# First-weight pieces of 512 columns, an early touch of the weight, and a gate on k's first exponential, in a fused attention and SiLU kernel

## The chip, the cores and the metric

One core of a Trainium2 chip runs the whole program. The metric is the device time of one execution in microseconds; the time before is the median of seven runs. A profiled execution, taken by the hardware profiler, gives the traces.

## The reference

```
# q, k, v: (8, 8, 576, 64) f32; w_in: (512, 2048); w_out: (2048, 512)
q_s = softmax(q, axis=-1)              # exp / sum over the head's 64 columns
k_s = softmax(k, axis=2)               # exp / sum over the 576 rows
kv  = einsum('bhsd,bhse->bhde', k_s, v)
o   = einsum('bhsd,bhde->bhse', q_s, kv)
x   = o.transpose(0, 2, 1, 3).reshape(4608, 512)
h   = x @ w_in
out = (h * sigmoid(h)) @ w_out         # (4608, 512) f32
```

## The kernel before

**Tiling.** Eight batches of 576 rows go through linear attention; the resulting 4608 rows of x go through the two-layer block in nine chunks of 512 rows (chunk 0's first layer covers the 576 rows of batch 0, as a part i=0 of 320 columns and a part i=1 of 256). The head dimension is packed in two halves, called cc, of four heads each.

**Attention of one batch b.** `load` brings q, k, v as f32 tiles qt, kt, vt. `exp` (L114, ACT) makes eq and ek in bf16. `qsum` (L133, L134, DVE) sums eq and inverts, `qnorm` (L141) multiplies. eq is turned into qT, by TensorE (`tr`, L159) for batch 0 and by a DMA transpose (L151) after that. `vcast` (L123, L125) converts v into vaug, which carries a column of ones, so that `kv` (L178) gives k's sums too. `kvcopy` scales the result into kvn, on DVE (L198) or on ACT (L196), as the plan's `ke` says. `xt` (L220) multiplies kvn and qT, and `xtcopy` (L236, L238) moves the product from PSUM to XT, which holds x transposed.

**The two layers.** For chunk 0 `mm1` (L251) forms one block fb of 128 hidden columns from four matmuls, and `act1` (L281) applies SiLU on ACT into GT. Block fb reads W1 at columns 128 fb to 128 fb + 127. `mm2` (L530) is chunk 0's second layer. Chunk 1 and half of chunk 2 use `mm1` too. The rest of the first layer, and the second layer from chunk 1 on, use a seven-product scheme (`product1`, L344, and `product`, L445), whose sums of inputs are made by `xsum` (XS), `vsum` (TX), `presum` (SW and GT, L400 to L406) and `wsum` (TW), and whose results are joined by `sum1` (L362 to L370) and `after` (L467 to L486).

**Order.** All instructions of an engine run in program order. The start is written out by hand (L554 to L636); after it, a list of steps is sorted by the positions that PLAN, STEADY and their neighbours give: `order` for the first layer, `y` for the second, `act`, `add` for ACT and DVE steps, `pb` for presums, `kc` for kvcopy, and so on. Each chunk has its own plan; chunks 3 to 7 share STEADY.

**Transfers.** q, k, v of batch 0 are issued by SP, in halves: q, q, k, v, k, v. The weights and batch 1's q, k, v are issued by POOL, whose queue writes its descriptors in software and converts the f32 weights to bf16 on the way. `WORDER` is their order; `load_w` issues one. The first weight is cut into six pieces, w10 to w15: four of 256 columns, then two of 512. They are held back by a gate: a copy of one element of vt into a scratch tile on POOL, so that POOL's queue stands until v's first half has landed:

```
WORDER = ['w11', 'w13', 'w10', 'w12', 'w14', 'w15', 'q', 'w21', 'w20', 'k', 'w22', 'v', 'w23']
GATE = ('vt', 0)
```

Before its first products are due, TensorE runs matmuls on a constant tile (`heat`, L591). The first two products of `order`, (3,0) and (2,0), start with the two inner blocks of XT's first half, before the second half is copied.

Of the kernel before, what the change touches and what calls it, by code (L numbers as in the profile page):

```python
# [9 lines left out]
BF16 = mybir.dt.bfloat16  # L10
# [2 lines left out]
AX = mybir.AxisListType  # L13


PLAN = {
    0: {'y': [31.0, 31.5, 33.5, 34.0, 34.0, 34.5, 35.0, 35.5, 36.0, 38.5, 40.0, 41.0, 42.0, 44.0, 45.5, 46.5], 'ex': [28.8, 28.3, 35.8, 30.3], 'qs': [38.0, 36.5], 'qn': [38.51, 38.01], 'vs': [31.5, 39.5], 'ks': [43.0, 40.5], 'kc': [46.01, 43.6], 'lq': 41.5, 'tp': 40.5, 'ox': [47.5, 47.5], 'oc': [47.51, 47.6], 've': [2, 1], 'order': [(3, 0), (2, 0), (0, 0), (0, 1), (3, 1), (5, 0), (6, 0), (4, 0), (2, 1), (1, 0), (7, 1), (1, 1), (11, 1), (8, 1), (6, 1), (12, 0), (11, 0), (14, 0), (10, 1), (4, 1), (12, 1), (7, 0), (8, 0), (5, 1), (13, 0), (10, 0), (9, 1), (13, 1), (15, 1), (9, 0), (15, 0), (14, 1)], 'ke': [1, 0], 'oe': [1, 1], 'qe': [1, 0], 'pad': 16},
    1: {'ex': [15.2, 17.22, 22.74, 19.26], 'qs': [18.0, 18.5], 'qn': [18.01, 19.1], 'vs': [24.0, 20.0], 'ks': [26.0, 22.0], 'kc': [27.01, 26.01], 'lq': 13.5, 'lk': 19.6, 'lv': 22.2, 'tp': 19.5, 'ox': [28.0, 28.0], 'oc': [28.51, 28.51], 've': [2, 2], 'pa': [10.9, 13.5, 14.0], 'pae': [0, 0, 0], 'ke': [0, 0], 'oe': [2, 0], 'std': 4, 'order': [], 'add': {}, 'act': {}, 's1': {0: 1, 1: 0, 2: 0, 3: 1}, 'sl': [2.5, 2.5, 2.0, 6.0, 4.5, 6.0, 6.0, 9.0, 8.0, 9.0, 10.5, 11.0, 12.5, 14.0, 15.0, 15.0], 'xs': [7.3, -20.9, 0.5, -6.5], 'xe': [0, 1, 1, 1], 'pad': 14, 'qe': [1, 0]},
    2: {'std': 2, 'order': [(3, 1), (3, 6), (2, 1), (2, 6), (3, 7), (3, 5), (2, 2), (2, 7), (3, 4), (3, 2), (2, 5), (2, 4), (2, 3), (3, 3)], 'y': [-12.5, -12.5, -11.5, -11.0, -11.0, -10.0, -10.0, -10.0, -9.0, -8.0, -5.5, -2.5, -2.0, -1.0], 'ex': [-1.207, -2.202, -0.08, 1.794], 'qs': [9.4, 3.4], 'qn': [11.41, 6.91], 'vs': [1.42, 11.4], 'ks': [19.4, 19.4], 'kc': [19.41, 19.41], 'lq': 19.95, 'lk': 14.762, 'lv': 26.91, 'tp': 12.9, 'ox': [19.9, 20.4], 'oc': [19.91, 20.91], 'sl': [4.5, 5.0, 2.5, 7.5, 5.0, 6.0, 10.0, 10.5], 'add': {(3, 6): 10.55, (3, 7): 12.55, (3, 3): 22.02, (3, 2): 16.02, (3, 1): 9.55, (3, 5): 13.55}, 'act': {(2, 3): 21.02, (3, 5): 17.02, (3, 3): 22.02, (2, 5): 18.55, (3, 4): 18.55, (2, 2): 18.02, (3, 1): 10.02, (2, 1): 11.55, (2, 6): 12.02, (3, 2): 17.55, (2, 4): 21.02}, 's1': {2: 0, 3: 1}, 'xs': [0.1, 1.1, 8.1, 8.1], 'pa': [19.45, 20.45, 20.95], 'ya': {5: -6.0, 3: 1.0, 4: -2.05}, 'm1': [0, 0], 'pb': [-14.4, -13.8, -13.9, -15.5, -9.5], 'xe': [0, 0, 0, 0], 'pae': [1, 1, 1], 'pbe': [0, 0, 0, 1, 0], 've': [1, 2], 'ke': [0, 1], 'oe': [1, 0], 'qe': [1, 0]},
}  # L20
STEADY = {'std': 0, 'order': [(0, 1), (0, 6), (0, 5), (0, 7), (0, 2), (1, 1), (0, 4), (1, 6), (0, 3), (2, 1), (1, 2), (1, 7), (1, 5), (2, 6), (1, 4), (1, 3), (2, 2), (2, 7), (2, 5), (2, 4), (3, 1), (3, 6), (2, 3), (3, 2), (3, 7), (3, 5), (3, 4), (3, 3)], 'y': [0.5, 1.5, 5.0, 6.0, 9.0, 9.5, 9.5, 12.5, 14.5, 18.0, 19.5, 22.5, 25.7, 28.402], 'ex': [3.798, 1.41, 3.92, 1.297], 'qs': [11.4, 6.9], 'qn': [12.41, 9.91], 'vs': [10.9, 12.92], 'ks': [19.4, 19.4], 'kc': [21.91, 20.41], 'lq': 8.95, 'lk': 23.9, 'lv': 24.41, 'tp': 17.4, 'ox': [23.4, 23.4], 'oc': [24.41, 26.41], 'sl': [], 'add': {(3, 6): 22.02, (0, 3): 8.02, (0, 2): 6.02, (0, 5): 5.02, (2, 2): 20.02, (1, 3): 15.55, (1, 4): 15.55, (2, 7): 17.55, (1, 2): 10.55, (0, 4): 8.02, (1, 1): 6.02, (2, 6): 14.55, (1, 6): 10.55, (3, 1): 20.55, (1, 7): 11.55, (3, 2): 24.02}, 'act': {(0, 2): 4.55, (0, 3): 10.02, (2, 5): 18.55, (0, 4): 9.02, (1, 5): 15.02, (3, 3): 27.404, (1, 3): 18.02, (0, 5): 5.02, (3, 4): 26.55, (1, 4): 17.02, (2, 4): 23.02, (2, 3): 23.02, (0, 6): 4.02, (1, 1): 8.02, (3, 6): 22.55, (0, 1): 2.55, (3, 5): 27.55, (2, 1): 13.02, (3, 2): 23.55, (3, 7): 27.02, (1, 7): 13.55, (2, 6): 15.02, (2, 7): 17.02, (1, 2): 12.55}, 's1': {0: 0, 1: 1, 2: 0, 3: 0}, 'xs': [0.296, 0.298, -0.227, 0.4], 'pa': [19.95, 27.407, 27.41], 'pb': [1.45, 1.96, 4.45, 5.46, 3.45], 'ya': {6: 8.0, 5: 18.5, 4: 22.95, 3: 28.852, 7: 14.5}, 'm1': [0, 0], 'xe': [0, 0, 1, 1], 'pae': [1, 1, 1], 'pbe': [0, 0, 1, 1, 1], 've': [1, 2], 'ke': [0, 1], 'oe': [0, 0], 'qe': [1, 1]}
for _t in range(3, 8):
    PLAN[_t] = STEADY
PLAN[8] = {'std': 0, 'order': [(0, 1), (0, 6), (0, 2), (0, 7), (1, 1), (0, 5), (0, 4), (0, 3), (1, 6), (1, 2), (1, 7), (1, 5), (1, 4), (2, 1), (1, 3), (2, 6), (2, 2), (2, 7), (2, 5), (3, 1), (2, 4), (2, 3), (3, 6), (3, 2), (3, 7), (3, 5), (3, 4), (3, 3)], 'y': [1.5, 2.0, 5.5, 8.5, 10.0, 11.0, 14.0, 15.0, 19.5, 22.0, 24.5, 25.8, 27.401, 27.406], 'sl': [], 'add': {(2, 7): 17.55, (3, 2): 24.02, (3, 7): 24.55, (3, 4): 26.55, (3, 1): 20.55, (2, 3): 22.55, (0, 2): 3.55, (0, 3): 8.02, (2, 4): 20.55, (1, 4): 14.02}, 'act': {(2, 1): 15.55, (3, 6): 24.02, (3, 4): 26.55, (2, 3): 24.55, (2, 4): 21.55, (1, 7): 14.02, (2, 6): 19.02, (0, 3): 10.02, (1, 5): 12.55, (0, 4): 8.02, (3, 5): 27.403, (1, 4): 15.02, (2, 7): 21.02, (3, 7): 25.55, (1, 6): 10.02, (1, 3): 15.55, (3, 2): 23.55, (2, 2): 19.02, (3, 1): 20.02, (0, 5): 7.55, (1, 1): 6.55}, 's1': {0: 1, 1: 0, 2: 1, 3: 1}, 'xs': [-0.71, -0.208, -0.207, 1.4], 'pa': [24.45, 27.45, 29.429], 'pb': [0.793, 3.96, 10.45, 8.46, 9.45], 'ya': {6: 10.0, 4: 27.401, 7: 15.45, 2: 11.95}, 'm1': [0, 0], 'xe': [0, 0, 1, 0], 'pae': [1, 1, 1], 'pbe': [0, 1, 0, 1, 0]}
PLAN[9] = {'y': [0, 1, 2, 3, 4, 5, 6, 7, 8, 9, 10, 11, 12, 13], 'ya': {}, 'm1': [0, 0], 'pb': [-0.201, -0.2, -0.2, 1.9, 2.9], 'pbe': [0, 0, 0, 0, 0]}
TXAT = [(0, (0, -10.0, 0, 0)), (0, (0, 16.0, 1, 0)), (1, (1, -24.5, 0, 1)), (1, (0, 20.5, 1, 0)), (2, (0, 25.5, 0, 1)), (2, (2, -28.0, 1, 0)), (3, (2, -25.0, 0, 0)), (3, (1, -12.5, 1, 0))]
TWAT = [(1, -7.0, 1), (0, 38.0, 0), (1, 3.5, 0), (0, 46.0, 0), (1, 9.5, 1), (1, 20.5, 0), (1, 10.0, 0), (0, 39.0, 0)]
WORDER = ['w11', 'w13', 'w10', 'w12', 'w14', 'w15', 'q', 'w21', 'w20', 'k', 'w22', 'v', 'w23']
GATE = ('vt', 0)
HV = (1, 0.0, 0)  # L30
JS = 5
STD = 0
START = {'qn': (0, 0), 'h': [3, 3, 2, 2], 'v': 0, 't': (0, 0, 0, 2), 'x': 1, 'o': 0, 'w': 4}

@with_exitstack
def kernel(
# [13 lines left out]
    nc = tc.nc  # L50
# [6 lines left out]
    NC = DM // 128  # L57
# [10 lines left out]
    glob = ctx.enter_context(tc.tile_pool(name="glob", bufs=1))  # L68
# [15 lines left out]
    warm = glob.tile([128, 512], BF16, name="warm")  # L84
    dummy = glob.tile([1, 1], FP32, name="dummy")
    gate = glob.tile([1, 8], FP32, name="gate")

    ld = ctx.enter_context(tc.tile_pool(name="ld", bufs=1))
    ap = ctx.enter_context(tc.tile_pool(name="ap", bufs=2))
# [5 lines left out]
    st = [dict() for _ in range(B)]  # L95
# [13 lines left out]
    def exp(b, src, dst, cc, js=(0, J)):  # L109
        if dst not in st[b]:  # L110
            st[b][dst] = ap.tile([128, J, NG * D], BF16, name=dst, bufs=1)
        js = slice(*js)
        o = st[b][dst][:, js, cc * 128:(cc + 1) * 128].rearrange("p j (g d) -> p j g d", d=D)
        nc.scalar.activation(out=o, in_=jgd(st[b][src], cc)[:, js], func=ACT.Exp)  # L114

    def vcast(b, cc, eng, gs=(0, 2)):
        if gs[0] == gs[1]:
            return
        gs = slice(2 * cc + gs[0], 2 * cc + gs[1])
        o = vaug.rearrange("p j (g e) -> p j g e", e=E1)[:, :, gs, 0:D]  # L120
        i = st[b]["vt"][:, gs, :].rearrange("p g (j d) -> p j g d", d=D)
        if eng is nc.scalar:
            eng.copy(out=o, in_=i)  # L123
        else:
            eng.tensor_copy(o, i)  # L125
# [167 lines left out]
    def xsum(t, i):  # L293
        V = ENG[PLAN[t]["xe"][i]]
        w = width(t)
# [57 lines left out]
    def sum1(t, g, k):  # L353
# [12 lines left out]
        if k == 1:  # L366
            if PLAN[t]["s1"][g]:
                nc.vector.tensor_scalar_mul(out=new("s1"), in0=o, scalar1=1.0)
# [182 lines left out]
    PSB = {"ring": 6, "ops": 2}  # L551


    nc.vector.memset(dummy, 0.0)  # L554
    nc.vector.memset(warm, 0.0)
    nc.scalar.activation(out=dummy, in_=dummy, func=ACT.Exp)
# [9 lines left out]

    def load_w(name):
        if name[:2] == "w1":
            f = slice(*((0, 256), (256, 512), (512, 768), (768, 1024), (1024, 1536), (1536, 2048))[int(name[2])])
            nc.gpsimd.dma_start(  # L570
                out=W1[:, :, f], in_=w_in[:, f].rearrange("(c p) f -> p c f", p=128)
            )
        elif name[:2] == "w2":
            i = int(name[2])
            nc.gpsimd.dma_start(
                out=W2[:, i * 4:(i + 1) * 4, :],
                in_=w_out[i * 512:(i + 1) * 512, :].rearrange("(fc p) o -> p fc o", p=128),
            )
        else:
            load(1, name + "t", {"q": q, "k": k, "v": v}[name], eng=nc.gpsimd)  # L580

    gx = st[0][GATE[0]]
    nc.gpsimd.tensor_copy(gate[:, 0:1], gx[0:1, 2 * GATE[1] + 1, 0:1])
    for name in WORDER[:START["w"]]:
        load_w(name)

    wps = ps.tile([128, 512], FP32, name="wps", tag="ops", bufs=PSB["ops"])

# [7 lines left out]
    for cc in range(2):  # L596
        exp(0, "qt", "eq", cc)
        qsum(0, cc)
        if cc == 0 or not SB["o"]:
            qnorm(0, cc, ENG[SB["qn"][cc]])  # L600
    exp(0, "kt", "ek", 0)
    vcast(0, 0, nc.scalar)
    exp(0, "kt", "ek", 1)
    for js in HALF:
# [77 lines left out]
    for t in range(NCH):  # L682
        p = PLAN[t]
# [4 lines left out]
        else:  # L688
# [4 lines left out]
            for i, (g, m) in enumerate(p["order"]):  # L693
                x = i + 4 * p["std"]
# [9 lines left out]
    for t in range(1, NCH):  # L704
        for i, (m, a) in enumerate(HALVES):
            x = PLAN[t + 1]["y"][i]
# [14 lines left out]
    for t in range(1, NCH):  # L721
# [5 lines left out]
        for i in range(5):  # L727
            n, h = ((0, 1), (1, 1), (2, 1), (3, 0), (3, 1))[i]
# [33 lines left out]
```

## Time and profile before

| | |
|---|---|
| median of 7 runs | 273.75 us (272.12 to 274.76) |
| profiled execution, its own time | 274.76 us |
| its span | 272.9 us |
| TensorE busy | 254.9 us, 93% of the span |
| DVE, ACT, POOL busy | 200.1, 190.3, 146.8 us |
| mean granted TensorE clock | 0.989 |
| DMA | 46.50 MB in 44014 packets, 170 GB/s over the span |
| POOL's queue (software) | 6096 packets, 7.73 MB, 13.4% of 16 engines' span |

A row of a timeline has the start, the duration, the engine, the line in the kernel, the operation, output and inputs, and how many were merged; in brackets stands how long the engine was idle before, and what ended that. In a row of stretches come the stretch, its length, the busy time of TensorE's matmuls, its weight loads, DVE, ACT and POOL (with the number of instructions that began in it), then the granted TensorE clock, the DMA engines' busy share and the GB/s that they wrote. Sizes of the weight transfers are those of the bf16 side: 256 KB for 256 columns.

### The profile page before, as it was taken

How to read it: one execution, taken by the hardware profiler on the slowest of the kernel's cores; microseconds unless marked ns; L12 is line 12 of the kernel's file. 1: busy time of each engine (PE TensorE's matmuls, PEld its weight loads, DVE VectorE, ACT ScalarE, POOL GpSimd, SP SyncE). 2: the span in 40 equal slices, each digit the busy share in tenths (PEclk: the TensorE clock that was granted, in tenths of full speed). 3: DMA queues.
4: the chain of work that ended last, by engine and by line, in shares of the span. 5: the costliest groups of instructions: out<-in, count | busy, mean ns of one | idle time of the engine just before them, and what ended most of it. 6: DMA issues, size and time to landing. Idle time of an engine off the chain costs nothing.

```text
span 272.9 us, 6537 instructions
## 1 busy us (share of the span) xinstructions
PE 254.9 (93%) x2668; PEld 199.0 (73%) x2668; DVE 200.1 (73%) x343; ACT 190.3 (70%) x317; POOL 146.8 (54%) x91
## 2 busy tenths in 40 slices
PE   8659999899898989999999999998999999999992
PEld 3337754355773768888888888886888887888882
DVE  2932548755878877978996899687978578898832
ACT  5666899668858888977997698759975457444300
POOL 1496209033301978884979397849594637603500
PEclk9997999999999999999999999999999999999998
DMA  7799998991598596578655966592442102110324
GB/s 246 279 162 274 251 336 171 290 389 26 174 263 322 54 336 227 191 147 272 233 155 124 303 219 131 127 308 89 101 94 51 39 13 67 41 38 14 80 67 115
DMA packets 44014, 46.50 MB, mean 170 GB/s; under 512 B 18640, under 2 KB 31952, under 8 KB 43984
## 3 DMA queue, kind: packets, MB, share of 16 engines
q1 hardware_dynamic: 37728, 38.22, 48.0%
q0 software_dynamic: 6096, 7.73, 13.4%
q8 instruction: 21, 0.34, 0.5%
q10 hardware_dynamic: 160, 0.13, 0.2%
q14 instruction: 9, 0.07, 0.1%
HBM read 36.70 MB, written 9.44 MB: 169 GB/s over the span
## 4 chain that ended last, share of the span: by engine, by line
PE 53%; DMA 15%; ACT 9%; DVE 8%; issue 6%; POOL 4%; SPq 3%; DVEq 0%; POOLq 0%; ACTq 0%
PE ops L445 21%; PE hps L344 19%; PE hps L251 10%; DMA kt<-in_k_dram 7%; DMA qt<-in_q_dram 3%; DVE zq L133 2%; DMA qT<-eq 2%; DMA W<-in_moe_w_in_dram 2%; ACT eq L114 2%; DVE u L362 2%; ACT L114 2%; ACT ek L114 2%; ACT L281 1%; ACT GT L281 1%; POOL eq L141 1%
## 5 line engine op out<-in xcount | busy, mean ns | idle before, releaser
L445 PEld LDWEIGHTS <-GT 128*128 128x128 bf16 x512 | 49.5, 98 | 8.4 <-issue 2.3
L344 PEld LDWEIGHTS <-TX 128*128 128x128 bf16 x416 | 40.2, 98 | 8.4 <-issue 3.1
L344 PE MATMUL hps<-XS,TX 128*128 128x256 bf16 x312 | 43.3, 273 | 1.7 <-DVE u L362 0.9
L362 DVE SCALAR_TENSOR_TENSOR u<-hps,u 128x512 f32<-128x512 f32 x52 | 35.8, 688 | 8.8 <-PE hps L344 6.1
L362 DVE SCALAR_TENSOR_TENSOR u<-hps,s 128x512 f32<-128x512 f32 x52 | 35.4, 681 | 8.9 <-PE hps L344 8.8
L445 PEld LDWEIGHTS <-SW 128*128 128x128 bf16 x384 | 37.3, 98 | 5.5 <-DVE SW L402 1.0
L251 PE MATMUL hps<-XT,W 128*128 128x320 bf16 (+3 forms) x224 | 37.5, 328 | 3.6 <-DMA W<-in_moe_w_in_dram 2.2
L386 ACT ACTIVATE GT<-u 128x512 bf16<-128x512 f32 x52 | 32.2, 630 | 9.8 <-DVE u L362 9.8
L251 PEld LDWEIGHTS <-W 128*128 128x128 bf16 x224 | 22.4, 101 | 18.3 <-issue 2.8
L406 POOL TENSOR_TENSOR SW<-GT,SW 128x1024 bf16<-128x1024 bf16 x12 | 26.1, 2171 | 14.7 <-DVE SW L402 14.7
L344 PEld LDWEIGHTS <-W 128*128 128x128 bf16 x312 | 30.4, 98 | 4.0 <-issue 0.2
L445 PE MATMUL ops<-TW,SW 128*128 128x256 bf16 x256 | 32.8, 273 | 0.5 <-DVE SW L402 0.5
L141 POOL TENSOR_TENSOR eq<-eq,rzq 128x1152 bf16<-128x1152 bf16 x11 | 23.6, 2144 | 17.7 <-DVE rzq L134 12.5
L445 PE MATMUL ops<-TW,GT 128*128 128x256 bf16 x256 | 32.7, 273 | 0.3 <-DVE u L467 0.3
L133 DVE TENSOR_REDUCE zq<-eq 128x18 f32<-128x1152 bf16 x16 | 21.5, 1342 | 15.6 <-ACT eq L114 15.6
L445 PE MATMUL ops<-W,GT 128*128 128x256 bf16 x256 | 31.7, 273 | 1.3 <-ACT s L475 1.3
L281 ACT ACTIVATE GT<-hps 128x192 bf16<-128x192 f32 (+4 forms) x72 | 26.0, 408 | 7.6 <-PE hps L251 6.3
L344 PE MATMUL hps<-XT,W 128*128 128x256 bf16 x208 | 30.4, 273 | 0.0
L400 POOL TENSOR_TENSOR SW<-GT 128x1024 bf16<-128x1024 bf16 x7 | 14.9, 2126 | 27.6 <-ACT GT L386 19.0
L404 POOL TENSOR_TENSOR GT<-GT 128x1024 bf16<-128x1024 bf16 x12 | 25.5, 2128 | 0.0
L114 ACT ACTIVATE ek<-kt 128x1152 bf16<-128x1152 f32 x16 | 18.4, 1159 | 8.0 <-DMA kt<-in_k_dram 8.0
L386 ACT ACTIVATE GT<-s 128x512 bf16<-128x512 f32 x26 | 16.4, 631 | 10.0 <-DVE s L362 10.0
(79 smaller groups left out, 394.5 us busy)
## 6 DMA issues: line engine op xcount, KB each, us to landing
qt<-in_q_dram SPq DMA_DIRECT2D x6, 1152.0 KB, 5.8
kt<-in_k_dram SPq DMA_DIRECT2D x6, 1152.0 KB, 6.4
vt<-in_v_dram SPq DMA_DIRECT2D x6, 1152.0 KB, 9.6
out_dram<-u SPq DMA_DIRECT2D x34, 64.0 KB, 3.3
W<-in_moe_w_out_dram POOLq DMA_DIRECT2D x4, 512.0 KB, 18.6
out_dram<-u SPq DMA_DIRECT2D x14, 128.0 KB, 2.7
qt<-in_q_dram SPq DMA_DIRECT2D x2, 576.0 KB, 4.1
kt<-in_k_dram SPq DMA_DIRECT2D x2, 576.0 KB, 8.0
```

Of the source, the lines that this page charges most:

```text
L114: nc.scalar.activation(out=o, in_=jgd(st[b][src], cc)[:, js], func=ACT.Exp)
L133: nc.vector.reduce_sum(out=st[b]["zq"][:, cc, js], in_=e, axis=AX.X)
L141: eng.tensor_tensor(out=e, in0=e, in1=r[:, :, :, None].to_broadcast([128, n, 2, D]), op=ALU.mult)
L251: nc.tensor.matmul(out=hps[:, 0:size], lhsT=W1[:, c, fb * 128:(fb + 1) * 128], rhs=XT[t][:, c, off:off + size], start=(c == 0), stop=(c == ...
L281: nc.scalar.activation(out=y, in_=hps[:, h], func=ACT.Silu)
L344: nc.tensor.matmul(out=o[:, f, :], lhsT=l(c, 2 * g + f), rhs=r(c), start=bool(first and f == 0 and c == 0), stop=(c == HK - 1), skip_group ...
L362: nc.vector.scalar_tensor_tensor(out=out, in0=o, scalar=1.0, in1=x, op0=ALU.mult, op1=ALU.add)
L386: nc.scalar.activation(out=y, in_=MP[t, g, x], func=ACT.Silu)
L400: V.tensor_add(S1[:, f], quad(t, 0, f, 1), quad(t, 1, f, 1))
L404: V.tensor_sub(quad(t, 0, f, 1), quad(t, 0, f, 0), quad(t, 0, f, 1))
L406: V.tensor_sub(S4[:, f], quad(t, 1, f, 0), S2[:, f])
L445: nc.tensor.matmul(out=o, lhsT=l(f), rhs=r(f), start=bool(first and (own or a == 0) and f == 0), stop=(f == HF - 1), skip_group_check=True,)
```

## The change

- The first weight is cut into four pieces of 512 columns, issued in the order of their columns.
- POOL's first instruction is a transfer of four columns of the first weight into a tile that nothing reads (`touch`), 512 runs of four elements.
- The gate copies an element of ek's first half, which ACT writes in the first exponential of k, and the gate and the weights' issue are placed behind that exponential in the program.
- The order of chunk 0's first-layer products follows the new pieces: all of fb 0 to 3 first, then 4 to 7, 8 to 11, 12 to 15.
- In STEADY, kvcopy of cc 0 goes from DVE to ACT (`ke`), and one presum's position changes from 5.46 to 4.46 (`pb`). In the program that moves two kvn scalings in each of four chunks.
- In chunk 8's plan one second-layer product comes half a step earlier, one join half a step earlier, one SiLU has a position of its own, and three presums come two steps later. DVE's L406 and L404 thereby stand behind three sums that they stood among.

```
+WCUT = ((0, 512), (512, 1024), (1024, 1536), (1536, 2048))
+WARM = 1
 PLAN[0]:
-  'order': [(3, 0), (2, 0), (0, 0), (0, 1), (3, 1), (5, 0), (6, 0), (4, 0), (2, 1), (1, 0), (7, 1), (1, 1), (11, 1), (8, 1), (6, 1), (12, 0), ...]
+  'order': [(3, 0), (2, 0), (0, 0), (0, 1), (3, 1), (2, 1), (1, 0), (1, 1), (5, 0), (6, 0), (4, 0), (7, 1), (6, 1), (4, 1), (7, 0), (5, 1), ...]
 STEADY:
-  'pb': [1.45, 1.96, 4.45, 5.46, 3.45], 'ke': [0, 1]
+  'pb': [1.45, 1.96, 4.45, 4.46, 3.45], 'ke': [1, 1]
 PLAN[8]:
-  'y': [..., 19.5, ...], 'add': {..., (1, 4): 14.02}, 'pb': [0.793, 3.96, 10.45, 8.46, 9.45]
+  'y': [..., 19.0, ...], 'add': {..., (1, 4): 13.55}, 'act': {..., (2, 5): 20.02}, 'pb': [0.793, 3.96, 12.45, 10.46, 11.45]
-WORDER = ['w11', 'w13', 'w10', 'w12', 'w14', 'w15', 'q', 'w21', 'w20', 'k', 'w22', 'v', 'w23']
-GATE = ('vt', 0)
+WORDER = ['w10', 'w11', 'w12', 'w13', 'q', 'w21', 'w20', 'k', 'w22', 'v', 'w23']
+GATE = ('ek', 0)
-START = {..., 'w': 4}
+START = {..., 'w': 3}
+    if WARM:
+        nc.gpsimd.dma_start(
+            out=touch, in_=w_in[:, 0:4].rearrange("(c p) f -> p c f", p=128)
+        )
     nc.vector.memset(dummy, 0.0)
...
-            f = slice(*((0, 256), (256, 512), (512, 768), (768, 1024), (1024, 1536), (1536, 2048))[int(name[2])])
+            f = slice(*WCUT[int(name[2])])
...
-    gx = st[0][GATE[0]]
-    nc.gpsimd.tensor_copy(gate[:, 0:1], gx[0:1, 2 * GATE[1] + 1, 0:1])
-    for name in WORDER[:START["w"]]:
-        load_w(name)
...
     exp(0, "kt", "ek", 0)
+    gx = st[0][GATE[0]]
+    gx = gx[0:1, 2 * GATE[1] + 1, 0:1] if GATE[0][1] == "t" else gx[0:1, 0, GATE[1] * 128:GATE[1] * 128 + 1]
+    nc.gpsimd.tensor_copy(gate[:, 0:1], gx)
+    for name in WORDER[:START["w"]]:
+        load_w(name)
     vcast(0, 0, nc.scalar)
```

## The prediction

> **What bounds the kernel now.** I read four views: the page's engine shares and slices, the chain of work that ended last, the timelines of the first 40 us by engine, and stretches of 1 us. Two rows of the page first.
>
> ```profile
> PE 254.9 (93%) x2668; PEld 199.0 (73%) x2668; DVE 200.1 (73%) x343; ACT 190.3 (70%) x317; POOL 146.8 (54%) x91
> PEclk9997999999999999999999999999999999999998
> ```
>
> TensorE is busy 93% of the span, so little is left but its holes, and its clock drops once, in the fourth slice (20.5 to 27.3 us). Both edits that look large (weight pieces, gate) lie just ahead of that. The chain in order of time shows what leads there:
>
> ```profile
> 10.31 1.30 POOL gate L583
> 11.61 1.62 POOL W L570 x2
> 13.22 6.35 DMA W<-in_moe_w_in_dram
> 19.62 13.62 PE hps L251 x96
> 33.27 1.75 ACT GT L281 x7
> 35.04 1.28 ACT L114
> ```
>
> Gate, weight issue, weight transfer, first-layer products of chunk 0, their SiLUs, the exponential's table. From 35.04 on ACT is packed until 48.4. TensorE's and ACT's timelines give the price of the late weight:
>
> ```profile
> 16.17 1.26 PE L251 MATMUL hps<-XT,W 128*128 128x320 bf16 x8
> 19.62 16.44 PE L251 MATMUL hps<-XT,W 128*128 128x320 bf16 x120 [2.19 <-DMA W<-in_moe_w_in_dram]
> 18.21 0.77 ACT L281 ACTIVATE GT<-hps 128x320 bf16<-128x320 f32 x2
> 20.37 1.43 ACT L281 ACTIVATE GT<-hps 128x320 bf16<-128x320 f32 x5 [1.39 <-PE hps L251]
> 22.43 0.44 ACT L281 ACTIVATE GT<-hps 128x320 bf16<-128x320 f32 x1 [0.62 <-PE hps L251]
> 23.50 0.44 ACT L281 ACTIVATE GT<-hps 128x320 bf16<-128x320 f32 x1 [0.63 <-PE hps L251]
> 24.55 10.47 ACT L281 ACTIVATE GT<-hps 128x320 bf16<-128x320 f32 x35 [0.62 <-PE hps L251]
> ```
>
> The 8 matmuls of w11 run at once; the third piece, w10, is awaited 2.19 us. ACT idles 1.39 + 0.62 + 0.63 + 0.62 = 3.26 us, first for the stall and then because TensorE runs at half clock:
>
> ```profile
> 0.00:11.50 11.50, 8.02 (x41) 3.47 (x44) 6.45 (x11) 6.14 (x6) 1.92 (x7) 1.00 0.83 301
> 12.00:13.00 1.00, 1.00 (x12) 0.66 (x11) 0.88 (x5) 0.91 (x1) 1.00 (x2) 1.00 0.08 30
> 19.00:20.00 1.00, 0.38 (x3) 0.31 (x4) 0.00 (x0) 0.00 (x0) 0.70 (x2) 1.00 1.39 187
> 22.00:23.00 1.00, 1.00 (x6) 0.54 (x5) 0.00 (x0) 0.44 (x1) 0.40 (x1) 0.50 1.25 205
> ```
>
> The last three columns are clock, DMA share and GB/s written. Clock 0.50 lasts from 21.0 to about 24.4. The 256-column pieces arrive at about 187 GB/s, the 512-column ones at 205; at 12 to 13 us the DMA is empty. The POOL and DVE timelines explain the gate:
>
> ```profile
> 10.28 1.33 POOL L583 COPY gate<-vt 1x1 f32<-1x1 f32 x1 [8.97 <-DMA vt<-in_v_dram]
> 11.55 4.65 POOL L570 DMA_DIRECT2D W<-in_moe_w_in_dram  x6
> 10.21 1.36 DVE L141 TENSOR_TENSOR eq<-eq,rzq 128x1152 bf16<-128x1152 bf16 x1
> ```
>
> **Weight pieces.** w10 now holds fb 0 to 3, all that the first 8 products use (order (3,0), (2,0), (0,0), (0,1), (3,1), (2,1), (1,0), (1,1)). It writes 512 KB: 2.56 us at 205 GB/s. Before, three 256 KB pieces (786 KB, w13 in the middle) had to land first: first bytes near 13.2, landing 19.6. With the same start, w10 lands near 13.2 + 2.6 + 0.5 (the rate is only 113 to 145 GB/s from 15 to 18 us) + 1 (last bytes to release, as 786 KB took 5.4 of 6.35 us) = 17.3. The products could start at 16.17, so a stall of about 1.1 us stays, against 2.19 in mid-stream, and w11 follows 2.6 us later while w10 feeds 4 x 0.53 + 4 x 0.43 = 3.8 us of matmuls (320 and 256 columns at 2.4 columns per ns, as the warm rows run: 4 x 256 columns in 0.44 us). No later piece is awaited. 32 products need 15.4 us: 17.3 to 32.7, against 36.06. The two saved issues (2 x 0.77 us on POOL) shorten nothing, as POOL runs ahead of the transfers. All four pieces end at 13.2 + 10.2 + 0.5 = 23.9, where w15 landed at 26.2 (DVE waits for it): the q, k, v and w_out transfers behind them on POOL's queue come at least 1 us sooner, so ACT's later needs (k at 41.9, v at 44.7) are met even if shifted 2 us.
>
> ACT then sets the end: its 13.55 us of SiLU work before 35.02 can run packed from 18.21 (the SiLU table load, 16.92 to 18.20, hides the stall). Removed: 3.26, less 0.5 us for small waits while TensorE is only just ahead: -2.7.
>
> **The clock.** The row says: a gap of 2.19 us, then 3.4 us at 0.50. The Trainium skill (TensorE: Matmul & The Clock Gate, Part 1) has the clock halved only after an idle window of about 3.4 us. By the rule the drop has another cause and would stay: TensorE's 29th product, which releases the exponential, comes at 17.3 + 13.9 + 1.7 = 32.9, ACT's end moves only to about 33.5, and the sum loses 0.8. By the row a gap half as long is safe, as one of 1.47 us at 10 to 11.5 us left the clock at 1.00. I follow the row.
>
> **Gate.** ek's first half ends at 8.74 + 1.16 = 9.90, v's first half lands at 10.25. So the gate's wait is 0.35 shorter. But its 1.33 us for one element ends 0.04 after the DVE product of 10.21 to 11.57. The skill (SBUF — State Buffer, on the shared port pair) says that a DVE instruction with two SBUF inputs blocks a GpSimd one that reads SBUF; the row agrees, and speaks against the edit: unless the copy starts before 10.21 it is held to 11.6 as before. By the wait alone the weight comes 0.35 sooner, by an escape 1.5, by the lock 0. The margin is 0.3 us and the touch delays k more than q, so I take 0. POOL's queue behind the gate is the weights, then q, k, v loads; all move with it. In the new order nothing else of POOL passes it.
>
> **Touch.** The 4 KB transfer has 512 runs of 16 bytes, first on POOL's queue: about 0.9 us (first weight issue 0.94) ahead of the identity, which TensorE needs at 8.67: hidden. But its packets share the DMA engines with q, k, v, saturated from 2 to 11.5 us, and those have no cover. Nearest row: 18640 packets under 512 B in 7 transposes of 5.5 us, so 512 cost 512 x 7 x 5.5 / 18640 = 1.1 us. Upper end: the software queue's mean, 13.4% x 16 x 272.9 / 6096 = 96 ns a packet, 512 / 16 x 96 = 3.1 us. Lower: -0.2, if it takes the first-issue surplus (0.94 less 0.77) off the weight. I take 1.1 for the last loads, and 0.6 for the DVE chain that leads to XT, since it starts from q's first half, which meets about half the packets.
>
> **Planner edits.** Four chunks move two kvn scalings (0.24 us apart) from DVE to ACT. DVE waits 1.27 us right after them, at 172.4; ACT has a 0.42 us wait two steps later, and xt starts 1.0 us after ACT would be done. Price 0, between -0.3 and +0.3 each. pb 5.46 to 4.46 leaves POOL's order alone: 0. In chunk 8 DVE's L406 and L404 move behind three sums; L404 would end near 242.6, its reader on TensorE starts 242.82: 0, up to +0.5.
>
> **Sum.** -2.7 + 0.6 = -2.1, in a profiled run of 274.76 (span 272.9). Beyond 53 us TensorE is the bound and the loads chain on buffers, so the shift carries. That run is 1.0 above the median of the 7 runs, 273.75; I apply the shift to the median: 271.65.
>
> **Rivals.** (1) Gate escapes the lock and the touch is free (-0.2): -2.7 - 0.2, w10 at 16.2: 270.8. For it: 0.3 us of margin. Against: k is third in the queue. (2) Half the gain is lost: the clock still drops (+0.8) or the touch reaches the XT chain with its full 1.1 (+0.5): -0.8, 273.0. (3) Slower: tiny packets at the start cost like the software queue's, or more. From 2.7 us of delay on q, k, v (84 ns a packet) the whole gain is gone; at half as much again as that mean, about 150 ns (assumed; no row has runs of 16 bytes), it is 4.8 us: +2.1, 275.9. Against: the transposes' packets cost 33 ns per engine by the same row (5.5 x 7 x 16 / 18640). Place: the wait of the first eq and ek on qt and kt.
>
> **Chances.** Likeliest 0.48, rival 1 0.17, rival 2 0.20, rival 3 0.15. Faster by over 0.5% (below 272.4; about what a measurement of this kernel can tell) 0.65, within 0.5% 0.20, slower 0.15. The likeliest case alone spans 270.8 to 272.5 (touch 0.2 to 1.1, waits 0 to 1); 269.9 to 274.4 adds rivals 1 and 2 and the planner's bounds.
>
> **To check.** Right: no TensorE wait on W after the first products, clock 1.00 at 20 to 25 us, ACT's table load near 33 instead of 35.04, a later q landing by about 0.5. Wrong: a gate copy ending well before DVE's second L141 (rival 1), a clock of 0.5 after 18 us (2), eq's first start past 6 us (3), or TensorE waits at kvn or SW in chunks 4 to 8.

## The result, and the profile after

The changed kernel takes 270.6 us (median of 27 runs, 268.45 to 272.86) against 273.26 us for the kernel before (64 runs, 270.86 to 277.56): a ratio of 0.9901, 95% interval 0.9880 to 0.9923, so 1.0% or 2.7 us faster. The medians are of all runs; the ratio leaves out those more than 1.5% above the fastest of their kernel. The forecast was 271.65, with -2.1 us against the median that it had, 273.75. Faster was the side forecast; the case that came true is rival 1 (the gate escapes the lock, the touch is free) more than the likeliest, as the steps below show.

The profiled execution has a span of 267.5 us, 5.4 less than the first profile of the kernel before. That is twice what the medians differ, because both profiles are off their medians: before's execution took 274.76 us where the median is 273.26, after's 269.25 where it is 270.6.

The page's rows for the engines and the clock:

```profile
PE 253.6 (95%) x2668; PEld 198.7 (74%) x2668; DVE 197.7 (74%) x335; ACT 191.4 (72%) x325; POOL 144.0 (54%) x90
PEclk9999999999999999999999999999999999999999
```

The clock's hole in the fourth slice is gone. The chain in order of time (start, duration, what) no longer has the weight in it. It starts with q's transfer, goes through DVE's preparation of XT, and enters the first-layer products at 15.66:

```profile
0.74 3.62 DMA qt<-in_q_dram
...
15.13 0.53 PE o L224 x8
15.66 13.95 PE hps L255 x112
29.61 0.02 issue
29.63 0.88 ACT GT L285 x3
30.51 0.02 issue
30.53 1.28 ACT L118
```

The last row, the table load for the second batch's exponentials, stood at 35.04. I use its start below as the mark of how far chunk 0 has got. The timeline of the same execution, the rows that answer to those shown of before:

```profile
1.25 0.93 POOL L559 DMA_DIRECT2D touch<-in_moe_w_in_dram  x1 [0.80 <-POOLq L754]
9.20 0.18 POOL L607 CAST gate<-ek 1x1 f32<-1x1 bf16 x1 [6.43 <-ACT ek L118]
9.32 3.01 POOL L578 DMA_DIRECT2D W<-in_moe_w_in_dram  x4
10.22 1.36 DVE L145 TENSOR_TENSOR eq<-eq,rzq 128x1152 bf16<-128x1152 bf16 x1
15.59 15.85 PE L255 MATMUL hps<-XT,W 128*128 128x320 bf16 x128
17.64 12.88 ACT L285 ACTIVATE GT<-hps 128x320 bf16<-128x320 f32 x43
```

All 128 matmuls run in one piece of 15.85 us (worked out: 15.4), with no wait on W. ACT's 43 SiLUs run packed; its four gaps, 3.26 us together, are gone. The gate's copy takes 0.18 us, before DVE's L145 begins. By 1 us stretches (clock, DMA share and GB/s written are the last three columns):

```profile
12.00:13.00 1.00, 1.00 (x15) 0.52 (x15) 1.00 (x6) 0.67 (x3) 1.00 (x2) 1.00 1.22 196
19.00:20.00 1.00, 1.00 (x10) 0.80 (x9) 0.00 (x0) 1.00 (x7) 0.75 (x1) 1.00 1.23 203
22.00:23.00 1.00, 1.00 (x10) 0.80 (x9) 0.00 (x0) 1.00 (x6) 1.00 (x1) 1.00 1.09 402
```

The hole in the transfers at 12 to 13 us (share 0.08) is filled, and the weight is through by 22, when q of the next batch (402 GB/s) takes over. That hole belonged to the late gate and not to the pieces: in the second profile of the kernel before, whose gate copy took 0.18 us, the same stretch has a share of 1.42 and 184 GB/s.

### The profile page after: what moved, and what is told of

The parts are those of the page before. It is cut to its first block, busy times and chain, and to the rows that moved or that the text cites. A ratio compares the mean times of both kernels' runs of the same rounds, so it can differ in the third digit from the quotient of the medians.

```text
span 267.5 us, 6537 instructions
## 1 busy us (share of the span) xinstructions
PE 253.6 (95%) x2668; PEld 198.7 (74%) x2668; DVE 197.7 (74%) x335; ACT 191.4 (72%) x325; POOL 144.0 (54%) x90
## 4 chain that ended last, share of the span: by engine, by line
PE 69%; DVE 10%; ACT 8%; DMA 6%; issue 2%; SPq 2%; DVEq 0%; ACTq 0%
PE ops L449 28%; PE hps L348 26%; PE hps L255 11%; DMA kt<-in_k_dram 5%; DVE zq L137 2%; ACT eq L118 2%; ACT L118 2%; ACT ek L118 2%; DVE eq L145 2%; DVE u L366 1%; PE o L224 1%; PE kvps L182 1%; DMA qt<-in_q_dram 1%; ACT L285 1%; SPq L155 1%
## 5 line engine op out<-in xcount | busy, mean ns | idle before, releaser
L255 PE MATMUL hps<-XT,W 128*128 128x320 bf16 (+3 forms) x224 | 35.6, 318 | 1.5 <-ACT GT L285 1.0
L348 PEld LDWEIGHTS <-W 128*128 128x128 bf16 x312 | 30.4, 98 | 4.1 <-issue 0.4
L255 PEld LDWEIGHTS <-W 128*128 128x128 bf16 x224 | 21.8, 98 | 14.9 <-issue 2.6
L145 POOL TENSOR_TENSOR eq<-eq,rzq 128x1152 bf16<-128x1152 bf16 x11 | 23.5, 2138 | 16.2 <-DVE rzq L138 11.0
L404 POOL TENSOR_TENSOR SW<-GT 128x1024 bf16<-128x1024 bf16 x7 | 14.9, 2127 | 27.6 <-ACT GT L390 15.3
L285 ACT ACTIVATE GT<-hps 128x64 bf16<-128x64 f32 (+4 forms) x72 | 25.3, 419 | 4.3 <-PE hps L255 3.0
```

The lines of the kernel that those rows point to most:

```text
L145: eng.tensor_tensor(out=e, in0=e, in1=r[:, :, :, None].to_broadcast([128, n, 2, D]), op=ALU.mult)
L255: nc.tensor.matmul(out=hps[:, 0:size], lhsT=W1[:, c, fb * 128:(fb + 1) * 128], rhs=XT[t][:, c, off:off + size], start=(c == 0), stop=(c == ...
L285: nc.scalar.activation(out=y, in_=hps[:, h], func=ACT.Silu)
L348: nc.tensor.matmul(out=o[:, f, :], lhsT=l(c, 2 * g + f), rhs=r(c), start=bool(first and f == 0 and c == 0), stop=(c == HK - 1), skip_group ...
L404: V.tensor_add(S1[:, f], quad(t, 0, f, 1), quad(t, 1, f, 1))
```

## The experiments

Theory A: the loss is the wait for w10 in mid-stream, and the order and size of the pieces mend it. Rivals: the gate's release does it; the touch does it; the planner's edits do it.

**Each part alone.** The first kernel has only the pieces, their issue order and the product order; the second only the gate on ek. In both the gate and the weights' issue stand behind k's first exponential in the program, as in the changed kernel, against which the edits are shown:

```
 GATE = ('vt', 0)      # pieces_only
-WARM = 1
+WARM = 0
 # STEADY and PLAN[8] as before

 GATE = ('ek', 0)      # gate_only
+WCUT = ((0, 256), (256, 512), (512, 768), (768, 1024), (1024, 1536), (1536, 2048))
 # WORDER, PLAN[0] order, STEADY, PLAN[8] as before; WARM = 0
```

> The kernel before with the four 512-column pieces and the product order that goes with them; gate on vt, no touch, old plan. Theory A (the wait for the first weight and the half clock after it are the loss, and the piece cut alone mends it): no TensorE wait on W after the first products, table load of the first exponential near 32.5 us instead of 35.0, about 2.0 us faster than before. Theory B (the gate's earlier release does it, the cut only follows): gate copy still 1.3 us long, first products wait for w10 until about 17.3, less than 0.8 us gained.

> The kernel before with the gate on ek's first half; six pieces, old order, no touch, old plan. Theory A: the six pieces arrive up to 1.5 us sooner, the 2.19 us wait for w10 shrinks below 1 us and the clock stays at 1.00, so this alone gains about 1.5 us and the two edits do not add up. Theory B: gate copy ends before DVE's second product (0.2 us instead of 1.33) and 2.0 us or more are gained. If a late k makes the gate miss the port, the copy lasts 1.3 us and nothing is gained.

Measured: pieces alone 0.9925 (0.9892 to 0.9958), 270.56 us against 272.63; gate alone 1.0006 (0.9972 to 1.0041), 272.85 us. Their timelines, first the pieces:

```profile
9.96 0.18 POOL L607 COPY gate<-vt 1x1 f32<-1x1 f32 x1 [8.65 <-DMA vt<-in_v_dram]
15.85 15.86 PE L255 MATMUL hps<-XT,W 128*128 128x320 bf16 x128
30.79 1.28 ACT L118 ACT_TABLE_LOAD   x1
```

Then the gate alone:

```profile
9.67 0.18 POOL L607 CAST gate<-ek 1x1 f32<-1x1 bf16 x1 [8.36 <-ACT ek L118]
18.61 15.11 PE L255 MATMUL hps<-XT,W 128*128 128x320 bf16 x120 [1.48 <-DMA W<-in_moe_w_in_dram]
32.69 1.28 ACT L118 ACT_TABLE_LOAD   x1
```

With the pieces there is no wait although the gate is the old one; with the new gate and the old pieces a wait of 1.48 us stays. Theory A holds for the pieces, with their issue order and the product order that goes with them; which of these two orders does how much was not tested. Its guess that the gate alone would gain 1.5 us fell: the old gate, too, lets go at 9.96 here. The clock stayed at 1.00 in the gate kernel despite the wait.

**Each small part taken away.** The changed kernel without the touch (`WARM = 0`), and with the old plans:

> The changed kernel without the touch. Theory A: the touch's packets cost 24 ns each and nothing waits for them, so no difference from the changed kernel (2.7 us faster than before, within 0.5). Theory B: the touch takes a first-use delay (in the changed kernel 3 us pass between its issue and its packets) off the first weight piece; without it w10 comes 1 us or more later than 15.5 and the gain falls below 2 us.

> The changed kernel with the old STEADY and chunk 8 plans (kvn scaling back on DVE, presums back). Theory A: no difference from the changed kernel (2.7 us faster than before, within 0.5), as the moved work lies beside a busy TensorE. Theory B: the planner's edits bring the 0.9 us that the profiled pair differs after chunk 0, so the gain falls to 1.8 us.

Measured: 0.9916 (0.9884 to 0.9948), 270.54 us, and 0.9918 (0.9887 to 0.9949), 270.62 us. Neither part can be told from nothing beside 0.9901; with intervals of this width a part worth less than about 1 us does not show. The timeline without the touch, then the touch's own answer in the changed kernel:

```profile
9.76 3.17 POOL L578 DMA_DIRECT2D W<-in_moe_w_in_dram  x4
16.15 15.85 PE L255 MATMUL hps<-XT,W 128*128 128x320 bf16 x128 [0.26 <-DMA W<-in_moe_w_in_dram]
31.09 1.28 ACT L118 ACT_TABLE_LOAD   x1
```

```profile
DMA to landing us min/median/max: 6.7/6.7/6.7
```

The touch lands 6.7 us after its issue at 1.25. Its 512 packets run from 5.15 to 7.56 us, at 24 ns each in the mean, so they begin when q's first exponential has started already: at 4.38 in both kernels. They do take room on the DMA engines (278 GB/s at 5 to 6 us, against 341 without the touch), but k's first exponential starts at 7.97 to 8.74 us in the seven profiles with the touch and at 7.82 to 8.74 in the seven without. What the touch gives is the first weight issue's surplus: four issues take 3.01 us with it and 3.17 without, 0.16 us. The wait of 0.26 without it is within what other draws of the changed kernel show.

**Order or size of the pieces.** The changed kernel with the six old pieces, issued in the order of their columns:

```
-WCUT = ((0, 512), (512, 1024), (1024, 1536), (1536, 2048))
+WCUT = ((0, 256), (256, 512), (512, 768), (768, 1024), (1024, 1536), (1536, 2048))
-WORDER = ['w10', 'w11', 'w12', 'w13', 'q', ...]
+WORDER = ['w10', 'w11', 'w12', 'w13', 'w14', 'w15', 'q', ...]
-START = {..., 'w': 3}
+START = {..., 'w': 4}
```

> The changed kernel with the six old pieces (256 columns for the first four) issued in the order of their columns. Theory A1 (the order of arrival is what counts: w13 no longer stands between the pieces that the first products need): as fast as the changed kernel, within 0.5 us. Theory A2 (the size counts: 256-column pieces come at 145 to 187 GB/s against 205): the first products wait about 0.6 us for W, the later ones not, and 0.5 to 1.0 us of the gain is lost.

Measured: 0.9944 (0.9906 to 0.9982), 271.43 us against 273.31. Timeline and one stretch:

```profile
17.08 15.85 PE L255 MATMUL hps<-XT,W 128*128 128x320 bf16 x128 [1.03 <-DMA W<-in_moe_w_in_dram]
32.02 1.28 ACT L118 ACT_TABLE_LOAD   x1
```

```profile
17.00:18.00 1.00, 0.92 (x7) 0.69 (x8) 0.00 (x0) 1.00 (x1) 0.42 (x1) 1.00 1.35 172
```

The order counts: it alone takes away the break in mid-stream, and its gain is clear of noise. Of the 2.7 us, 1.9 are there without the larger size by the medians, 1.5 by the ratio. The size probably counts too, but its share of the time is not shown, since the intervals of the two kernels overlap. What the traces show is the rate: from 13 to 18 us this kernel writes 128 to 172 GB/s, and the changed kernel with the old plans (no_plan), whose weights are issued at nearly the same time (10.10 against 10.05 us), 197 to 219. The two pieces of 256 columns reach the products 1.03 us late; there the first one of 512 is not awaited at all (0 to 0.76 us in the four profiles of the changed kernel).

**The port.** The gate of the changed kernel copies from rzq, which DVE finishes just before L145:

```
-    gx = gx[0:1, 2 * GATE[1] + 1, 0:1] if GATE[0][1] == "t" else ...
+    gx = st[0]["rzq"][0:1, 1, 0, 0:1]
```

> The changed kernel, with the gate copying one element of rzq's second half, which DVE writes just before its second normalizing product (L145). Theory A (the port is shared): the copy starts within 0.1 us after L145 does, and lasts until L145 ends, about 1.3 us instead of 0.18; the weights' issue starts near 11.6 instead of 9.3 to 10.1, the first products wait about 1 us for W, and about half of the gain goes (1.0 to 2.0 us faster than before). Theory B (the 1.33 us of the kernel before were something of the first copy on POOL, not the port): the copy lasts 0.2 us, and little is lost.

Measured: 0.9967 (0.9931 to 1.0004), 271.6 us against 273.31.

```profile
10.31 1.36 DVE L145 TENSOR_TENSOR eq<-eq,rzq 128x1152 bf16<-128x1152 bf16 x1
10.34 1.37 POOL L607 COPY gate<-rzq 1x1 f32<-1x1 f32 x1 [7.57 <-DVE rzq L138]
17.15 15.85 PE L255 MATMUL hps<-XT,W 128*128 128x320 bf16 x128 [1.31 <-DMA W<-in_moe_w_in_dram]
32.09 1.28 ACT L118 ACT_TABLE_LOAD   x1
```

The one-element copy starts 0.03 us after L145, and ends 0.04 us after it: 1.37 us instead of 0.18. This bears out what the Trainium skill (SBUF — State Buffer, Who interferes with whom) states of a DVE instruction with two SBUF inputs and a GpSimd one that reads SBUF. The weight then comes 1.31 us late. Of the gain of 2.7 us, 1.7 are left by the medians and 0.9 by the ratio; the interval does not overlap with that of the changed kernel, so a loss is there, but its size is loosely known.

**More profiles of both.** Three more of each kernel, unchanged:

> The kernel before once more, for a second profile of it. If the profile shown first is typical: gate copy 1.3 us, wait for w10 near 2.2 us, clock 0.5 for 3.4 us, table load at 35.0. If it is a slow draw, as its 274.76 against a median of 272.6 to 273.3 suggests: the gate copy may start ahead of DVE's product and take 0.2 us, the wait is near 1.5 us, the clock stays at 1.00 and the table load is near 33 us.

> The changed kernel once more, for a second profile. No wait on W after the first products in any draw, table load at 30.5 to 31.1 us; the gate copy 0.18 us unless k's first half lands after 8.9 us.

> The kernel before, third profile. Theory A (the wait for w10 is there in every draw, the port lock and the half clock only in some): wait 1.5 to 2.2 us, table load 33 us with a gate copy of 0.2 us and a full clock, up to 35 us with a copy of 1.3 us and a clock of 0.5. Theory B (the wait itself comes only with the lock): no wait when the copy takes 0.2 us.

> The kernel before, fourth profile; as for the third. The gate copy lasts 1.3 us exactly where v's first half lets it start after DVE's second L141, and 0.2 us where it starts before.

> The changed kernel, third profile. Theory A: no wait for W above 0.3 us, clock 1.00 to 25 us, table load 30.5 to 31.1 us, gate copy 0.18 us. Theory B: draws with table loads of 32 us or more turn up here as well.

> The changed kernel, fourth profile; as for the third. After chunk 0, the lead over the second profile of the kernel before stays between 2 and 4.5 us.

The three profiles of the kernel before, in this order: the gate copy, the first-layer products with their wait for W, ACT's SiLUs that began after a gap, and the table load:

```profile
9.91 0.18 POOL L583 COPY gate<-vt 1x1 f32<-1x1 f32 x1 [8.60 <-DMA vt<-in_v_dram]
19.08 15.02 PE L251 MATMUL hps<-XT,W 128*128 128x320 bf16 x120 [2.02 <-DMA W<-in_moe_w_in_dram]
19.84 6.11 ACT L281 ACTIVATE GT<-hps 128x320 bf16<-128x320 f32 x21 [1.22 <-PE hps L251]
26.30 6.76 ACT L281 ACTIVATE GT<-hps 128x320 bf16<-128x320 f32 x21 [0.35 <-PE hps L251]
33.08 1.28 ACT L114 ACT_TABLE_LOAD   x1
...
9.86 0.18 POOL L583 COPY gate<-vt 1x1 f32<-1x1 f32 x1 [8.55 <-DMA vt<-in_v_dram]
20.22 14.77 PE L251 MATMUL hps<-XT,W 128*128 128x320 bf16 x120 [3.20 <-DMA W<-in_moe_w_in_dram]
20.97 12.97 ACT L281 ACTIVATE GT<-hps 128x320 bf16<-128x320 f32 x42 [2.41 <-PE hps L251]
33.96 1.28 ACT L114 ACT_TABLE_LOAD   x1
...
9.33 0.18 POOL L583 COPY gate<-vt 1x1 f32<-1x1 f32 x1 [8.02 <-DMA vt<-in_v_dram]
17.44 1.59 PE L251 MATMUL hps<-XT,W 128*128 128x320 bf16 x12 [0.70 <-DMA W<-in_moe_w_in_dram]
19.42 13.35 PE L251 MATMUL hps<-XT,W 128*128 128x320 bf16 x108 [0.39 <-DMA W<-in_moe_w_in_dram]
20.17 11.56 ACT L281 ACTIVATE GT<-hps 128x320 bf16<-128x320 f32 x37 [0.66 <-PE hps L251]
31.75 1.28 ACT L114 ACT_TABLE_LOAD   x1
```

And the changed kernel, its third and fourth profile:

```profile
16.55 15.85 PE L255 MATMUL hps<-XT,W 128*128 128x320 bf16 x128 [0.76 <-DMA W<-in_moe_w_in_dram]
31.48 1.28 ACT L118 ACT_TABLE_LOAD   x1
...
15.97 15.86 PE L255 MATMUL hps<-XT,W 128*128 128x320 bf16 x128 [0.29 <-DMA W<-in_moe_w_in_dram]
30.91 1.28 ACT L118 ACT_TABLE_LOAD   x1
```

All eight side by side (us):

| | gate copy | wait for W | table load | span |
|---|---|---|---|---|
| before 1 (shown first) | 1.33 | 2.19 | 35.04 | 272.9 |
| before 2 | 0.18 | 2.02 | 33.08 | 271.8 |
| before 3 | 0.18 | 3.20 | 33.96 | 271.1 |
| before 4 | 0.18 | 0.70 + 0.39 | 31.75 | 268.9 |
| after 1 (shown first) | 0.18 | 0 | 30.53 | 267.5 |
| after 2 | 0.18 | 0 | 30.55 | 268.1 |
| after 3 | 0.18 | 0.76 | 31.48 | 269.1 |
| after 4 | 0.18 | 0.29 | 30.91 | 268.4 |

The means of the table loads are 33.46 and 30.87: 2.6 us apart, and the medians of the times differ by 2.7. So, as far as four profiles of each kernel can tell, the gain is made by 31 us and the rest of the program passes it on.

Of the expectations, these held: before 2 takes the faster course that was expected if the first profile is a slow draw (a wait of 2.02 us where 1.5 was put down, a table load at 33.08); the gate copy took 0.18 us in each of the three further profiles of before, where it started ahead of DVE's second L141 (at 9.91, 9.86 and 9.33, against 10.18, 10.34 and 10.11); and before 2 stands 2.2 us behind after 4 at the table load and 3.4 at the end. These were too narrow: a wait of 1.5 to 2.2 us in every draw of before (3.20 in one, 0.70 + 0.39 in another), and for after no wait above 0.3 and a table load by 31.1 (0.76 and 31.48 in after 3). Theory B of before 3, that the wait comes only with the lock, fell: all three waited without it. And before 4, a plain draw of the old kernel, ended 0.2 us ahead of after 3. The runs spread by 4 to 7 us, so a pair of profiles does not measure this change.

## Why the prediction was right or wrong

**w10's wait: right in kind.** The products are no longer broken off, no later piece is awaited, and 32 products run in 15.85 us (15.4 were worked out with 2.4 columns per ns; the row named for it, 4 x 256 columns in 0.44 us, gives 2.33). They start at 15.59 to 16.55 us where 17.3 was worked out, after 0 to 0.76 us of wait where 1.1 was. Two terms of that sum fell away. The gate escaped the port, as in rival 1. And the 0.5 us for a slow stretch (113 to 145 GB/s from 15 to 18 us) was a misreading: the low rate went with the 256-column pieces, and the changed kernel writes 203 to 213 GB/s there.

**ACT sets the end: right, its size too small for the draw it was read from.** 35.04 to 30.53 in the first pair is 4.51, where 2.7 was taken: 3.26 of gaps, all gone; 0.57 from an earlier start of the SiLUs (18.21 to 17.64), since k and v landed sooner in that execution; and about 0.7 more. Of that, 0.3 is one SiLU that the new order puts behind the table load (44 before it became 43; it is paid there). The remaining 0.4 goes with fewer bursts: a SiLU that stands alone takes 0.44 us where packed ones follow each other every 12.88 / 43 = 0.30 us. That split is read from the rows, not tested.

**The shift was applied to the wrong base: wrong.** The step "that run is 1.0 above the median; I apply the shift to the median" took a shift out of an execution whose chunk 0 was the slowest of four, and put it on the typical one. Its table load, 35.04, stands 1.6 us behind the mean of the four, 33.46. In the typical execution ACT's gaps are not 3.26 us but 1.98, the mean of 3.26, 1.57 (1.22 + 0.35), 2.41 and 0.66, and at the table load only 2.6 us were to be had. So the shift was too small for the execution it was read from (2.7 against 4.51), and that execution was too slow for the median it was put on; the two errors nearly cancel. That 2.7 fits the 2.6 is luck.

**Touch, +0.6: wrong, it costs nothing that shows.** The working let q's first half meet about half of the touch's packets. In the trace they begin at 5.15 us, when that half has landed: q's first exponential starts at 4.38, against 4.37 before. They take 24 ns each, where the transposes gave 33 and rival 3 assumed 84 to 150. Removing the touch changed nothing that the intervals can tell. This 0.6 us is about what the forecast, -2.1 against a measured -2.7, was short of.

**Clock: the row that I followed does not carry a rule.** I read a gap of 2.19 us as enough to halve the clock. Before 2 and before 3 have gaps of 2.02 and 3.20, and the third's stretches after the gap are at full clock:

```profile
20.00:21.00 1.00, 0.78 (x7) 0.61 (x8) 0.00 (x0) 0.03 (x1) 0.54 (x1) 1.00 1.26 207
21.00:22.00 1.00, 1.00 (x11) 0.86 (x9) 0.00 (x0) 1.00 (x4) 0.65 (x2) 1.00 1.26 209
```

The skill's page (TensorE: Matmul & The Clock Gate, Part 1) names an idle window of about 3.4 us that runs freely. A gap of 3.20 without a drop fits it, one of 2.19 with a drop does not. No gap length here predicts the drop, which came in one of four profiles of the old kernel and in none of the four of the changed one; its cause stays open. Two sums around it were off: by the working's own figures a drop costs 33.5 less 32.3 (35.02 - 2.7), so 1.2 us and not 0.8, and rival 2's -0.8 adds both of the terms that it joins by "or".

**Gate: the mechanism right, the odds wrong.** The lock is real (0.18 against 1.37 us, made on purpose above). I took it as the typical course and gave an escape a margin of 0.3 us; the copy escaped in four of four profiles of the changed kernel, and in three of four of the old one. So the new gate brought nothing that shows by itself (1.0006), though the lock, made on purpose in gate_on_rzq, cost 1.0 us by the medians and 1.8 by the ratios.

**Planner's edits, 0: right** within what no_plan can tell (0.9918 against 0.9901, about 1 us either way).

**The signs set down in advance.** No wait after the first products, and a clock of 1.00 at 20 to 25 us, came true. The table load came at 30.5 to 31.5 and not near 33, and q's landing did not move by 0.5. Of the signs of being wrong, one came: the gate copy ends 0.3 to 0.8 us ahead of DVE's second L145 in all four profiles (9.38 against 10.22 in the first), the sign of rival 1.

## What to carry to other kernels

Cut and order a first load by what its first consumers read: the first piece should hold all that the engine can work on until the second one lands, and nothing else should stand in between. A profile is one draw: before a stall is priced from it, see how far its own time stands from the median, and take a second profile if the price depends on things that differ from one execution to the next (a gate that meets a port, the landing of a transfer's last bytes, a clock that drops). And do not forecast a shift from an extreme draw onto the median.

## What the runs showed of the hardware

- The wait for the same third piece went from 0.70 to 3.20 us in four profiles of one kernel, while the weights' issue started at 9.45 to 11.55. An earlier gate explains part of it; before 3 issued at 9.98 and waited longest. What holds the last bytes up was not settled.
- A software-queue transfer of 4 KB issued at 1.25 us, while the other queue filled the engines from 2 us on, landed 6.7 us later, and 7.6 us in the second profile of the same kernel.
- In all eight profiles the rest of the program, from the product of kvn and qT for the second chunk on (at 51.68, 49.72, 50.61 and 48.39 us before, 47.18, 47.20, 48.14 and 47.74 after), took 220.3 to 222.1 us. In these profiles nothing later takes the gain back, but this rest scatters by more than half of it.
